# A two-layer SSM/MLP training step on one core: the opening in one written order, half-row forms, and moved gates

## The chip, the cores and the metric

The kernel runs on one core of a Trainium2 chip. The metric is the device time of one launch in microseconds, the median over repeated launches. The kernel before takes 688.93 us (688.62 to 689.18 over three launches). Five engines work side by side: PE (matrix products; its weight loads are listed as PEld), DVE and ACT (elementwise work, reductions, copies out of PSUM, the accumulator memory), POOL (a few small operations and the issue of many transfers) and SP (the issue of transfers only). Each engine executes its own instructions in order and waits on semaphores for what other engines or transfers must have finished.

## The reference

The reference runs four residual blocks on a sequence of 2048 rows with 448 channels in bf16, alternating a long convolution with an MLP, and returns the output and the gradients for eight inputs:

```python
def _A_ref(q, k, v, shift_k, ssm_k, ssm_D):      # D = 448, S = 2048
    k_shift = sum(k_pad[:, t:t + S, :] * shift_k[:, ks - 1 - t] for t in range(4))
    kv = k_shift * v
    y = irfft2(rfft2(pad(kv)) * rfft2(pad(ssm_k)))[:S] + kv * ssm_D
    return q * y

def _B_ref(x, w1, w2):                           # F = 1792
    return einsum(silu(einsum(x, w1)), w2)

x = A_q
x = x + _A_ref(_layernorm(x), A_k, A_v, A_shift_k, A_ssm_k, A_ssm_D)
x = x + _B_ref(_layernorm(x), B_w1, B_w2)
x = x + _A_ref(_layernorm(x), ...)               # same weights
x = x + _B_ref(_layernorm(x), ...)
# outputs: x and the gradients of A_q, A_k, A_v, A_shift_k, A_ssm_k, A_ssm_D, B_w1, B_w2
```

The long convolution's y does not depend on x, only on k, v and the filters, so it is computed once and used in both layers.

## The kernel before

The kernel has three stages.

**Opening** (`_ssm_prefix`). It computes y with a Fourier transform of length 4096 written as matrix products in two stages, 128 by 16 by 2. In order:

- The filter ssm_k (called K) is loaded in four blocks of channels (`KPARTS`), turned on PE (`k_turn`), multiplied with the first-stage matrix `M1sb` (`k_stage1`), turned again in seven groups of 16 blocks (`turn`; groups 5 and 6 by DMA transposes on SP's queue, L444) and multiplied with the second-stage matrix (`spec_k`, `P_`). The result `Ka` is the spectrum of K. It is stored to DRAM (`spec_K`), and a second copy with the real and imaginary halves swapped is made by four SBUF to SBUF transfers for each 2048 columns (`_swap_halves_dma`, L289). Stores and swaps are issued by POOL (`Q` in the written order).
- k is turned (`kT`, L450) and convolved with the four taps of shift_k by products with diagonal matrices (`conv`, L469). Each diagonal is the identity times one column of shift_k, built by sixteen DVE operations (L433). ACT copies the result out (L472), POOL stores it to DRAM (`KS_d`), DVE multiplies it with v (L475), and the product kv goes through the first stage (`stage1_kv`, L485).
- kv is turned in seven groups (`Z_`), taken through the second stage in fourteen blocks of 1024 (`F_`), stored (`spec_KV`), multiplied with the two copies of K's spectrum (`M`, L573), and taken back through the inverse second stage (`V`, L260 and L261). Every PSUM result is copied to SBUF by ACT or DVE (lines L116 and L117 are these copies for all callers).
- `ys` (L604) applies the inverse first stage, eight steps, and leaves y in `Ysb`. It is issued by the main part.

Inside the opening, an order written out by hand (`PRODUCTS`) fixes PE, ACT, DVE and POOL from the ninth block of `spec_k` on; what stands before that is ordered by the planner, which also chooses the copying engine from running loads (`bal.pick`). PSUM gives the opening four tiles of two banks, used in turn.

On SP's queue the opening issues the input loads, the two DMA transposes of K, two DMA transposes that bring w2 turned into `w2T` (L454 and L455), the load of the inverse matrix `Minvsb`, and a tile of grad_out (`gb0`). POOL's queue also carries the loads of w1 and w2 (L563, L564, L568), traced behind the store of the kv spectrum's blocks 9 and 10.

**Main part** (`Main.run`). The rows are handled in four chunks of 512. For each chunk it runs the norms, gates and MLPs forward and then the gradients back. The generators are: `Hh` and `H` (x times w1, with silu and a raw copy `Dall` for its slope), `O` (times w2, added to the residual `X` by DVE, L855), `G` (gradient times w2 turned, copied to `ghT` by ACT or by DVE as `dv` says), `N` (gradient times w1 turned, and the norm's gradient), `T` (turning a tile for the next product). `gate` (L722) multiplies y with the normed tile and adds the residual. `fwd0(c)` norms and gates the chunk c for the first layer; `fwd0_end` finishes its second norm. PE's order here is the order of the text; the other engines are ordered by the planner, with hints: `issue_after` puts an instruction behind another on its engine, `high_priority` moves it ahead. For chunks 1 and 2 the products are woven by one pattern, with L the remaining steps of `fwd0_end`:

```python
weave("OOLOOGOGOGOGGOGTG", O=o, G=g, L=self.norm, T=self.T(...))
```

**Closing** (`_ssm_suffix` and `Jobs`). The gradients of the convolution and the weight gradients of both MLP matrices. `Jobs.last` computes the last block of w1's gradient in two halves of 224 columns, each copied by ACT, turned on PE by `flush` and stored.

Of the kernel before, what the change touches and what calls it, by code (L numbers as in the profile page):

```python
# [17 lines left out]
P = 128  # L18
S = 2048
D = 448  # L20
# [101 lines left out]
PRODUCTS = """  # L122
P9 P10 P11 P12 p9a p10d p11a P13 p12d P8 p8a Z0 Q5 p13d Z1 z0d Z2 z1a Q6 F0 z2d F1 f0a F2 f1d F3 f2a F4 Q4 M0 F5 f3a Z4
f4a Z6 z4d f5a z6d F8 f8a F9 M1 F12 F13 f9a Z5 M2 f12a V0 z5d f13a Z3 v0a F11 z3yd z3xd F7 f11a M3 F6 f7a F10 V1 M4 f6a
V2 f10a M6 V3 v1a M5 V4 v2a M11 V5 v3a V6 M10 v4a V11 M12 v5a V10 M13 v6a V12 v11a M7 V13 v10a M8 V7 v12a M9 V8 v13a v8d
V9 v7a v9a
# [16 lines left out]
def kernel(  # L143
# [33 lines left out]
    k.KS_d = dram.tile([2, P, J, D // 2], BF16, name="KS_d")  # L177
# [87 lines left out]
def _fft_inv_stage2_half(k, pa, pb, B1, ci, psum, cnd):  # L265
    nc = k.nc
    pv = psum.tile([P, 2, 8, 64], FP32, name="ps_v", **k.pt["v"])
    for i in range(8):
        for src, g, first in ((pa, G_IAC, True), (pb, G_IBC, False)):
            for r in range(2):  # L270
                ri = slice(64 * r, 64 * r + 64)
                nc.tensor.matmul(pv[:, r ^ (ci & 1), i, :], lhsT=src[ri, i * P:(i + 1) * P], rhs=k.Gsb[ri, g, ri], start=first, stop=not first)  # L272
    out = (B1[:, :, 32 * ci:32 * ci + 32].rearrange("p q (i h s) -> p h i q s", h=2, s=2) if cnd
           else B1[:, 8 * ci:8 * ci + 8, :].rearrange("p i (q h s) -> p h i q s", h=2, s=2))
    _copy(nc, k.bal.pick(1024), out, pv[:].rearrange("p h i (q s) -> p h i q s", s=2))
# [45 lines left out]
def _ln_steps(k, pool, c, src, si, n_g):  # L321
# [4 lines left out]
    for tl in range(4):  # L326
        k.tc.keep_in_program_order(nc.vector.bn_stats(out=st[:, tl, :], in_=src(tl)))
# [5 lines left out]
        yield  # L333
    for tl in range(4):
        k.tc.keep_in_program_order(nc.vector.tensor_scalar(out=n_g[:, tl, :], in0=src(tl), scalar1=mv[:, tl, 0:1], scalar2=r[:, tl:tl + 1], op0=ALU.subtract, op1=ALU.mult))
        yield
# [6 lines left out]
def _ssm_prefix(k):  # L343
# [4 lines left out]
    with ExitStack() as es:  # L348
# [6 lines left out]
        k.M1sb = k.wk.tile([P, 16, 2, P], BF16, name="M1sb", tag="WX")  # L355
# [8 lines left out]
        kT = k.wk.tile([DC, 4, ND, 4, 129], BF16, name="kT", tag="W1")  # L364
        w2o = k.wk.tile([P, 2 * S + ND * 4 * DC], BF16, name="ksd", tag="W2")
        ksb = [w2o[:, i * S:(i + 1) * S] for i in range(2)]
        ksb += [_hd(k, [P, S], "K_sb")[:] for i in range(2)]
        diag = w2o[:DC, 2 * S:].rearrange("p (c j d) -> p c j d", c=ND, j=4)
        kn = k.wk.tile([P, J, D], BF16, name="k_n", tag="WY")
        vn = k.wk.tile([P, J, D], BF16, name="v_n", tag="WB")  # L370
        skc = spec.tile([DC, ND, 4], FP32, name="skc")
        skb = spec.tile([DC, ND, 4], BF16, name="skb")
# [3 lines left out]
        nc.scalar.dma_start(out=skb[:], in_=k.A_shift_k.rearrange("(c p) j -> p c j", p=DC))  # L376
        m1f = k.M1sb[:].rearrange("p a c k -> p (a c k)")
        for h in range(2):
            for lo, hi in KPARTS[2 * h:2 * h + 2]:
                nc.sync.dma_start(out=ksb[lo // P][:hi - lo], in_=k.A_ssm_k[lo:hi, :])  # L380
            nc.sync.dma_start(out=m1f[:, 2048 * h:2048 * h + 2048], in_=k.m1_h.ap()[:, 2048 * h:2048 * h + 2048])
# [17 lines left out]
        nc.gpsimd.tensor_copy(skc[:], skb[:])  # L399
        def k_turn(lo, hi):  # L400
            n = hi - lo
            kview = ksb[lo // P][:n].rearrange("p (n1 n2) -> p n2 n1", n2=16)
            pt = psum.tile([P, 2, 1024], BF16, name="ps_kt", **a_)
            pv = pt[:, :, 0:8 * n].rearrange("p g (i d) -> p g i d", d=n)
            for i in range(16):
                nc.tensor.transpose(pv[:, i // 8, i % 8, :], kview[:, i, :], k.ident[:n, :n])
            for g, e in enumerate((nc.vector, nc.scalar)):
                last = _copy(nc, e, Kt[:, 8 * g:8 * g + 8, lo:hi], pv[:, g])
                bal.add("act" if g else "dve", 0.9 if g else 0.69)
                if g == 0:  # L410
                    k.kt_copy = last

        def k_stage1(lo, hi, pairs):
            for n2 in pairs:
                ps = psum.tile([P, 2, 2, 256], FP32, name="ps_s1", **k.pt["s1"])
                if n2 == 0:
                    nc.vector.tensor_tensor(out=Kt[0:1, 0, lo:hi], in0=Kt[0:1, 0, lo:hi], in1=Drow[:, lo:hi], op=ALU.add)
                for w in range(2):
                    for c in range(2):
                        nc.tensor.matmul(ps[:, w, c, :hi - lo], lhsT=k.M1sb[:, n2 + w, c, :], rhs=Kt[:, n2 + w, lo:hi], start=True, stop=True)  # L420
                _copy(nc, bal.pick(4 * (hi - lo)), A1K[:, lo // 2:hi // 2, :, n2:n2 + 2, :].rearrange("p b c w s -> p w c b s"),
                      ps[:, :, :, :hi - lo].rearrange("p w c (b s) -> p w c b s", s=2))

        for lo, hi in ((0, 256), (256, D)):
            for plo, phi in KPARTS[lo // P:lo // P + 2]:
                k_turn(plo, phi)
# [1046 lines left out]
```

## Time and profile before

| what | value |
|---|---|
| median of the launches | 688.93 us |
| the profiled execution, its own time | 687.9 us |
| span in the trace | 686.1 us |
| PE busy | 665.3 us, 97% |
| DVE, ACT, POOL busy | 70%, 63%, 15% of the span |
| opening, up to the first product of `ys` | 84.06 us |
| PE idle in the opening | 8.2 us |
| PE idle between 140 and 500 us | 7.0 us |

The span is the time from the first to the last instruction in the trace; the device time has a little more around it. A busy time is the union of an engine's instructions. In a line such as `L889 PE MATMUL ps_n<-w1T,ghT 128*128 128x448 bf16 x448`, L889 is the line of the kernel, then come engine, operation, result and inputs by name, shapes and count. A name with buffers loses its numbers. DMA times run from issue to landing.

### The profile page before, as it was taken

To read this page: it belongs to the slowest core of one execution; us is meant where nothing else is said; L and a number is where in the kernel's file an instruction comes from. 1 tells how busy PE (TensorE), PEld (TensorE's weight loads), DVE (VectorE), ACT (ScalarE), POOL (GpSimd) and SP (SyncE) were. 2 spreads that over 40 slices of the span, in tenths; PEclk is the share of its full clock that TensorE was granted. 3 is DMA by queue.
4 is the path that set the end of the run, shared out by engine and by line. 5 is a ranking of instruction groups with operands and counts; after the bars stand their busy time and mean duration, and the time that the engine had idled before them with its cause. 6 is when DMAs were issued, how large, how long until landed. Compare 5 with 4: busy or idle time off the path is not lost.

```text
span 686.1 us, 14467 instructions
## 1 busy us (share of the span) xinstructions
PE 665.3 (97%) x5844; PEld 362.3 (53%) x5879; DVE 482.2 (70%) x1133; ACT 429.7 (63%) x528; POOL 104.6 (15%) x177
## 2 busy tenths in 40 slices
PE   8989999999999899999899999999999999999997
PEld 6876755554444344444444444544555555555666
DVE  5779954677879858898588874843937554528992
ACT  5988987888758668678477685123634543653431
POOL 1047320110010100101001000010111211102311
PEclk9999999999999999999999999999999999999999
DMA  8999989499788767598776799859599988956981
GB/s 316 248 278 316 342 191 227 112 228 258 191 241 228 219 163 193 123 250 231 182 162 193 218 241 375 241 173 205 200 238 354 324 274 323 351 173 223 324 308 42
DMA packets 203956, 162.60 MB, mean 237 GB/s; under 512 B 153505, under 2 KB 184244, under 8 KB 203122
## 3 DMA queue, kind: packets, MB, share of 16 engines
q1 hardware_dynamic: 190806, 113.35, 61.7%
q0 software_dynamic: 11088, 39.84, 17.1%
q10 hardware_dynamic: 1996, 8.49, 3.8%
q8 instruction: 46, 0.75, 0.4%
q14 instruction: 20, 0.16, 0.1%
HBM read 66.05 MB, written 54.60 MB: 176 GB/s over the span
## 4 chain that ended last, share of the span: by engine, by line
PE 77%; DVE 11%; ACT 5%; DMA 3%; issue 2%; POOL 1%; DVEq 0%; POOLq 0%
PE ps_d L1115 25%; PE ps_n L889 11%; PE ps_o L850 9%; PE ps_g L681 9%; PE ps_h L681 7%; PE ps_v L272 2%; PE ps_g L685 2%; PE ps_h L685 2%; DMA spec_K<-KAB 2%; DVE ln_st L309 1%; ACT KAB L116 1%; DVE lb_v L1063 1%; DMA KAB<-KAB 1%; PE ps_gK L1398 1%; PE ps_y L604 1%
## 5 line engine op out<-in xcount | busy, mean ns | idle before, releaser
L1115 PEld LDWEIGHTS <-dstat 128*128 128x128 bf16 x928 | 87.1, 98 | 75.7 <-issue 4.0
L889 PE MATMUL ps_n<-w1T,ghT 128*128 128x448 bf16 x448 | 94.5, 353 | 0.0
L850 PE MATMUL ps_o<-w2sb,aT 128*128 128x448 bf16 x448 | 89.2, 353 | 1.8 <-DVE X L855 1.8
L116 ACT CAST ghT<-ps_g 128x1024 bf16<-128x1024 f32 (+1 forms) x54 | 48.3, 899 | 60.9 <-PE ps_g L685 46.8
L681 PE MATMUL ps_h<-nT,w1sb 128*128 128x512 bf16 (+1 forms) x410 | 83.0, 336 | 2.1 <-DVE Dall L117 0.8
L681 PE MATMUL ps_g<-nT,w2T 128*128 128x512 bf16 x317 | 77.9, 379 | 1.6 <-ACT Dall L116 0.4
L889 PEld LDWEIGHTS <-ghT 128*128 128x128 bf16 x448 | 42.4, 98 | 45.3 <-issue 4.7
L850 PEld LDWEIGHTS <-aT 128*128 128x128 bf16 x448 | 43.2, 98 | 41.8 <-issue 3.5
L681 PEld LDWEIGHTS <-w1sb 128*128 128x128 bf16 x420 | 39.1, 98 | 37.1 <-issue 8.2
L1063 DVE SCALAR_TENSOR_TENSOR lb_v<-lb_u,n 128x448 bf16<-128x448 bf16 x60 | 37.2, 621 | 27.6 <-ACT lb_u L905 27.2
L833 ACT ACTIVATE aT<-ps_h 128x1024 bf16<-128x1024 f32 (+1 forms) x48 | 44.2, 922 | 19.7 <-PE ps_h L681 11.5
L116 ACT CAST Dall<-ps_h 128x1024 bf16<-128x1024 f32 (+2 forms) x60 | 54.8, 913 | 0.0
L843 ACT ACTIVATE Dall<-Dall 128x1024 bf16<-128x1024 bf16 (+1 forms) x48 | 53.3, 1186 | 0.1
L681 PEld LDWEIGHTS <-w2T 128*128 128x128 bf16 x336 | 31.3, 98 | 40.9 <-issue 5.9
L314 POOL TENSOR_TENSOR rstd<-ln_ve,mhalf 128x2 f32<-128x2 f32 (+1 forms) x24 | 19.6, 818 | 183.7 <-DVE ln_ve L313 183.7
L1115 PE MATMUL ps_d<-X,dstat 128*128 128x448 bf16 x224 | 47.6, 353 | 0.0
L1115 PE MATMUL ps_d<-go,dstat 128*128 128x448 bf16 x224 | 47.2, 353 | 0.0
L1115 PE MATMUL ps_d<-n3m,dstat 128*128 128x448 bf16 (+1 forms) x240 | 47.0, 340 | 0.0
L1115 PE MATMUL ps_d<-n1m,dstat 128*128 128x448 bf16 (+1 forms) x240 | 46.5, 340 | 0.0
L116 ACT CAST A1g<-ps_v 128x1024 bf16<-128x1024 f32 x14 | 14.9, 1064 | 36.5 <-PE ps_v L272 36.5
L855 DVE TENSOR_TENSOR X<-X,ps_o 128x448 bf16<-128x448 bf16 x32 | 19.5, 611 | 18.4 <-PE ps_o L850 18.2
L905 ACT ACTIVATE lb_u<-ps_n,rstd 128x448 bf16<-128x448 f32 x32 | 20.5, 639 | 16.8 <-PE ps_n L889 13.0
(210 smaller groups left out, 1111.9 us busy)
## 6 DMA issues: line engine op xcount, KB each, us to landing
dstat<-a_d SPq DMA_DIRECT2D x28, 512.0 KB, 5.0
dstat<-g_d SPq DMA_DIRECT2D x28, 512.0 KB, 5.4
a_d<-turned SPq DMA_DIRECT2D x16, 512.0 KB, 3.0
g_d<-turned SPq DMA_DIRECT2D x16, 512.0 KB, 3.0
a_d<-turned SPq DMA_DIRECT2D x16, 384.0 KB, 2.7
g_d<-turned SPq DMA_DIRECT2D x16, 384.0 KB, 2.8
spec_K<-KAB POOLq DMA_DIRECT2D x7, 512.0 KB, 6.3
KAB<-KAB POOLq DMA_DIRECT2D x28, 128.0 KB, 5.1
```

Source lines behind the costliest of these rows:

```text
L116: return nc.scalar.copy(out, in_)
L314: nc.gpsimd.tensor_tensor(out=r[:, lo:hi], in0=ve[:, lo:hi], in1=k.mhalf[:, lo:hi], op=ALU.pow)
L681: self.nc.tensor.matmul(ps, lhsT=w[:, b, ft * P:(ft + 1) * P], rhs=x[:, b], start=(start and b == 0), stop=(stop and b == bs[2]))
L685: self.nc.tensor.matmul(ps, lhsT=w[sl, b, ft * P:(ft + 1) * P], rhs=x[sl, b], start=start, stop=stop)
L833: self.last_silu = nc.scalar.activation(aT[hh][:, o:o + hi - lo, :], ps(lo, hi), ACT.Silu)
L843: self.nc.scalar.activation(dT[hh][:, o:o + n, :], dT[hh][:, o:o + n, :], ACT.Derivative_silu)
L850: nc.tensor.matmul(po[:, :D], lhsT=aT[ft // 7][:, ft % 7, tl * P:(tl + 1) * P], rhs=self.w2sb[:, ft, :], start=(ft == 0), stop=(ft == NF - 1))
L855: self.last_o = nc.vector.tensor_tensor(out=X[:, t, :], in0=X[:, t, :], in1=po[:, :D], op=ALU.add)
L889: nc.tensor.matmul(pns[tl][:, :D], lhsT=gh[h][:, ft % 7, tl * P:(tl + 1) * P], rhs=self.w1T[:, ft, :], start=(ft == 0), stop=(ft == NF - 1))
L905: nc.scalar.activation(u0[:], pn[:, :D], ACT.Identity, scale=k.rstd[2 * L + 1][:, t:t + 1], accum_out=cp[:, tl, 0:1])
L1063: nc.vector.scalar_tensor_tensor(out=v[:], in0=u0, scalar=-1.0 / D, in1=n_t, op0=ALU.mult, op1=ALU.mult, accum_out=cp[:, 1:2])
L1115: self.nc.tensor.matmul(ps[:, cols], lhsT=st[:, t, :], rhs=mov[:, t, cols], start=(first and t == 0), stop=(last and t == NT - 1))
```

## The change

- `PRODUCTS` becomes `OPENING`: 272 entries that fix the order of the whole opening behind its first loads, on PE, ACT, DVE, POOL and SP. A capital letter is PE work, a DVE product, a transfer or a norm step; a small letter is the copy out of PSUM, with `a` or `d` for ACT or DVE at its end. The planner's balance between the two copying engines is gone from there.
- Half-row forms (`h` in an entry): a turn or an inverse product is done as pairs of 64-row products (`turned`, `V_`, `_fft_inv_half`). All seven turns of K, two of four of k, six of seven of kv and three of fourteen inverse products have this form.
- The two DMA transposes of K leave SP; PE turns all seven groups.
- The convolution works on half rows too: k is turned in blocks of 128 channels, the diagonals are 64 wide, and each product has 64 rows and 64 columns. The channels are split 256 and 192 in place of 224 and 224. Two broadcast products on DVE build all diagonals. The convolved k is stored in whole rows (`KS_d`), and the closing reads it so.
- w2's DMA transposes come in nine pieces: seven of 256 rows for three blocks, two of 896 rows for the fourth. The inverse matrix and the tile of grad_out follow them on SP.
- The loads of w1 and w2 are traced when the eighth of the eight kv stores has been.
- Main part: the gate and the statistics of the next chunk move out of `fwd0` into `fwd0_end`, behind a residual add; `weave` gets a second L; the load of x for the following chunk moves there too. `G` copies with ACT alone for chunks 1 and 2. In the first chunk the second turned tile is copied by DVE, and another group of tiles has its own PSUM banks.
- Closing: `last` takes 336 columns first and makes the remaining 112 already turned, copied by DVE and stored without a turn.

The core of the diff:

```diff
-PRODUCTS = """
-P9 P10 P11 P12 p9a p10d p11a P13 p12d P8 p8a Z0 Q5 p13d Z1 z0d Z2 z1a Q6 F0 z2d F1 f0a F2 f1d F3 f2a F4 Q4 M0 F5 f3a Z4
...
+OPENING = """
+A0 a0xd A1 a1xd a1ya B01 a0yd b01a G0 G1 B03 b03a A2 a2d B02 A3 D0 B06 b06d B04 b02a a3a B15 b15d B17 T1 t1d b04a T0
+t0d b17a B16 b16a B05 b05a T2h D1 t2d C01 c01a B10 b10d B11 b11a O01 C02 c02a O02 m01 T3h t3d B07 b07a B14 b14a C12
...
+z1d S111 s111d P10 p10a N6 Q4 N7 S110 Z0h z0d Z3h s110a P5 Q6 Z6h z3xa z3yd p5a Q2 F2 f2a F7 z6d M2 F4 F6 f6d F13 f7a
+M7 f4a F12 F0 f13a U13 F1 W1 W2 W4 W0 Q5 M6 f12a f0a Z5 f1a V7 Z4h v7a z5d F3 f3a z4d U6 M13 V2 v2a F10 f10a F9 f9a F5
+M3 f5a V6 U4 v6a F8 f8a U7 M12 V13 v13a F11 f11a M1 U2 V3h U0 v3a V12 M4 V1 M9 M0 V4 V0 v12a M11 v1a v4a v0a V9h V11
+M5 v9a V5 M10 U11 V10 M8 V8h v11d v5a v8a v10d U9
 """
-            for j in range(4):
-                nc.vector.tensor_scalar(out=diag[:, dc, j, :], in0=k.ident[:DC, :DC], scalar1=skc[:, dc, j:j + 1], scalar2=None, op0=ALU.mult)
+        def G_(r):
+            n, rs = 3 + r, slice(64 * r, 64 * r + 64)
+            nc.vector.tensor_tensor(out=diag[rs, 0:n].rearrange("p c j d -> p (c j) d"),
+                                    in0=k.ident[rs, rs].rearrange("p (o d) -> p o d", o=1).broadcast_to((64, 4 * n, 64)),
+                                    in1=skb[rs, 0:n].rearrange("p c (j o) -> p (c j) o", o=1).broadcast_to((64, 4 * n, 64)), op=ALU.mult)
+        def turned(key, name, srcs, half):
+            if half:
+                pt = bank(key, [P, 2, 16, 64], name, BF16)
+                for i in range(16):
+                    _turn64(k, pt, i, srcs(i))
...
-        for g in range(5, 7):
-            nc.sync.dma_start_transpose(out=Z[:, 16 * g:16 * g + 16, :], in_=A1Kf[:, 16 * g:16 * g + 16, :].rearrange("p a b -> p (a b)"))
-                    for t in range(4):
-                        nc.tensor.matmul(pc[:, u, e * DC:(e + 1) * DC], lhsT=src, rhs=diag[:, 2 * h + e, t, :], start=(t == 0), stop=(t == 3))
+                        for r in range(2):
+                            if (e, r) in at:
+                                rs = slice(64 * r, 64 * r + 64)
+                                nc.tensor.matmul(pc[:, at[e, r], u, :], lhsT=src[rs], rhs=diag[rs, e, q, :], start=(q == 0), stop=(q == 3))
-        nc.sync.dma_start_transpose(out=k.w2T[:, 0:3, :], in_=k.B_w2[:, 0:384])
-        w2t = nc.sync.dma_start_transpose(out=k.w2T[:, 3:4, :], in_=k.B_w2[:, 320:448])
+        def W(i):
...
+                for lo in range(0, F, 256):
+                    nc.sync.dma_start_transpose(out=k.w2T[:, 0:3, lo:lo + 256], in_=k.B_w2[lo:lo + 256, 0:384])
...
+                for lo in range(0, F, 896):
+                    nc.sync.dma_start_transpose(out=k.w2T[:, 3:4, lo:lo + 896], in_=k.B_w2[lo:lo + 896, 320:448])
+        def U_(lo):
+            hi = min(x for x in (2, 4, 6, 7, 9, 11, 13, 14) if x > lo)
+            nc.gpsimd.dma_start(out=k.SPEC_d["KV"][:, lo * 1024:hi * 1024], in_=zkv(lo * 1024, hi * 1024))
+            stored.add(lo)
+            if len(stored) == 8:
+                ...
+                nc.gpsimd.dma_start(out=k.w1sb[:, 0:3, :], in_=k.B_w1[0:384, :].rearrange("(c p) f -> p c f", p=P))
+        with tc.manual_schedule(engines={e.engine for e in (nc.tensor, nc.scalar, nc.vector, nc.gpsimd, nc.sync)}):
@@ main part
-            self.a_fwd(c, 0, xc, n00, ((0, 4),))
+            _ln(k, self.ch, c, xc, 0, n00)
-            norm = _ln_parts(k, self.ch, c, self.xs(c), 1, n01, ((0, 4),))
-            next(norm)
-            self.norm = self.fwd0_end(c, norm, n01)
+            self.norm = self.fwd0_end(c, xc, n00, n01)
+    def fwd0_end(self, c, xc, n00, n01):
+        norm = _ln_parts(self.k, self.ch, c, self.xs(c), 1, n01, ((0, 4),))
+        with self.tc.issue_after(self.last_o.ins) if c > 1 else nullcontext():
+            self.gate(c, xc, n00)
+            next(norm)
+        if c < 3:
+            self.x_load(c + 1)
+        yield
-        hs = [self.Hh(0, 0, nT, aT, dT1, 0, (1, 3), (1,)), self.Hh(0, 0, nT, aT, dT1, 1)]
+        hs = [self.Hh(0, 0, nT, aT, dT1, 0, (1, 2), (2,)), self.Hh(0, 0, nT, aT, dT1, 1)]
-            self.transp_half(self.n0[0][1], nT, GBLK, 1)
+            self.transp_half(self.n0[0][1], nT, GBLK, 1, nc.vector)
-                g = self.G(gT, gh2, dv=(1, 4))
+                g = self.G(gT, gh2, dv=(1, 4) if c == 3 else ())
-                    weave("OOLOOGOGOGOGGOGTG", O=o, G=g, L=self.norm, T=self.T(self.n0[c + 1][1], nT, GBLK))
+                    weave("OOLOOLGOGOGOGGOGTG", O=o, G=g, L=self.norm, T=self.T(self.n0[c + 1][1], nT, GBLK))
@@ closing, Jobs.last
+        cols = slice(0, 3 * DC)
...
+                nc.tensor.matmul(ps[:DC, 0:P], lhsT=movs[i]()[:, t, 3 * DC:D], rhs=sts[i][:, t, :], start=(i == 0 and t == 0), stop=(i == 1 and t == NT - 1))
...
+        nc.vector.tensor_copy(o7[:, 3], ps[:DC, 0:P])
```

More of the change, by code (lines that the diff above doesn't have):

```diff
@@ L434, in _ssm_prefix, with a @@
[L434 to L443 removed]
+        def a(part, s, e):
+            lo, hi = KPARTS[part]
+            n = hi - lo
+            pv = live["a", part][:, :, 0:8 * n].rearrange("p g (i d) -> p g i d", d=n)
+            gs = {"": slice(0, 2), "x": slice(0, 1), "y": slice(1, 2)}[s]
+            _copy(nc, e, Kt.rearrange("p (g i) d -> p g i d", g=2)[:, gs, :, lo:hi], pv[:, gs])
@@ L539, in Q, with Z_ @@
             _swap_halves_dma(k, KAB[:, 0, :], Ka, lo, hi)
-        def Z_(g):
-            pt = live["z", g] = psum.tile([P, 16, P], BF16, name="ps_tr", **a_)
-            for i in range(16):
-                nc.tensor.transpose(pt[:, i, :], B1[:, 16 * g + i, :], k.ident[:])
-        def z(g, part, eng):
-            lo, hi = (8 * part, 8 * part + 8) if g == 3 else (0, 16)
-            _copy(nc, eng, block(g, lo, hi), live["z", g][:, lo:hi, :])
+        def Z_(g, half):
+            turned(("z", g), "ps_tr", lambda i: B1[:, 16 * g + i, :], half)
```

357 lines of the change are left out of this document (180 added, 177 removed).

## The prediction

> **What bounds the kernel now.** First the page's head and busy times, then the table of stretches:
>
> ```profile
> span 686.1 us, 14467 instructions
> PE 665.3 (97%) x5844; PEld 362.3 (53%) x5879; DVE 482.2 (70%) x1133; ACT 429.7 (63%) x528; POOL 104.6 (15%) x177
> ```
>
> ```profile
> 0.00:84.06 84.06, 75.90 (x1100) 61.47 (x1107) 67.53 (x95) 69.60 (x73) 30.95 (x64) 1.00 1.04 299
> 30.00:42.00 12.00, 11.42 (x191) 9.74 (x190) 9.24 (x17) 9.94 (x12) 3.25 (x6) 1.00 1.25 182
> 70.00:84.06 14.06, 13.33 (x243) 12.33 (x241) 13.55 (x13) 13.38 (x15) 5.27 (x10) 1.00 1.00 343
> 140.00:500.00 360.00, 353.05 (x2094) 164.71 (x2118) 271.28 (x767) 234.88 (x295) 31.23 (x48) 1.00 0.80 215
> ```
>
> The columns are length, then PE, PEld, DVE, ACT, POOL, the granted clock, DMA share, GB/s. Over the whole span PE idles 686.1 - 665.3 = 20.8 us. Of that, 84.06 - 75.90 = 8.2 us lie in the opening, which ends at 84.06 where ps_y starts, and 360 - 353.05 = 7.0 us in the main part. In the opening PE, ACT and DVE are busy 75.9, 69.6 and 67.5 us: three engines close together, PE first. From 70 us on DVE and ACT are full as well. The clock is 1.00, so the throttle has no part in it. The main part is PE end to end; only its PE waits and its work can give anything.
>
> The chain of waits (start, length, what) shows a second pace-maker in the opening, the transfers that swap the spectrum's halves:
>
> ```profile
> 18.67 3.73 PE ps_kT L450 x64
> 56.03 6.30 DMA spec_K<-KAB
> 69.63 7.34 DMA KAB<-KAB
> 83.00 1.02 ACT A1kv L116
> 84.06 6.74 PE ps_y L604 x32
> ```
>
> The last swap lands at 69.63 + 7.34 = 76.97; seven microseconds of products and copies later ps_y starts. So the end is set by engines and by DMA almost together.
>
> **The opening, priced by groups of instructions.** Groups of the opening, forms apart (count | busy, mean ns | idle before):
>
> ```profile
> L469 PE MATMUL ps_cv<-ksd,kT 112*128 112x112 bf16 x256 | 13.9, 213 | 0.4 <-ACT KAB L116 0.3
> L544 PE MATMUL ps_tr<-ident,A1kv 128*128 128x128 bf16 x112 | 7.1, 219 | 0.3 <-ACT KAB L116 0.2
> L232 PE MATMUL ps_tr<-ident,KAB 64*128 64x64 bf16 x160 | 3.0, 190 | 0.2 <-issue 0.2
> L260 PE MATMUL ps_v<-Gpre,pab 128*128 128x128 bf16 x112 | 13.2, 219 | 0.2
> L472 ACT CAST ks_kv<-ps_cv 128x896 bf16<-128x896 f32 x8 | 7.3, 914 | 3.8 <-PE ps_cv L469 3.8
> L116 ACT CAST KAB<-ps_s 128x1024 bf16<-128x1024 f32 x12 | 12.1, 1041 | 1.2 <-PE ps_s L251 0.7 <-PE ps_s L485 0.2 <-PE ps_s L420 0.2
> L116 ACT COPY KAB<-ps_tr 128x2048 bf16<-128x2048 bf16 x3 | 5.6, 1890 | 0.0
> L117 DVE CAST KAB<-ps_s 128x1024 bf16<-128x1024 f32 x10 | 11.9, 1217 | 1.6 <-PE ps_cv L469 1.2 <-PE ps_s L420 0.4
> L117 DVE COPY ZkvB<-ps_tr 128x2048 bf16<-128x2048 bf16 x3 | 3.6, 1218 | 0.4 <-PE ps_tr L544 0.4
> L433 DVE TENSOR_SCALAR ksd<-ident,skc 112x112 bf16<-112x112 bf16 x16 | 2.8, 242 | 0.0
> ```
>
> PE. A half-row transpose of 64x64 advances at 3.0 us / 160 = 0.019 us, because the two row halves run side by side; a full one at 7.1 / 112 = 0.063. With these two paces: the convolution's 256 products (13.9 us) become 4 x 64 + 4 x 48 = 448 half-row products of 64 columns, 8.4 us: -5.5. The key's 64 transposes (3.73 us) become 32 full and 64 half: 2.0 + 1.2 = 3.2, -0.5. Seven turns of K in place of five (the two DMA turns go): 224 half transposes for 160, +1.2. Seven turns of kv: one full, six half: 1.0 + 3.6 for 7.1, -2.5. Three of fourteen inverse products half-row: each 0.6 us for 13.2 / 14 = 0.94, -1.0. Together -8.3. What it costs is the change of form, which this trace shows in the main part:
>
> ```profile
> 95.60 1.48 PE L681 MATMUL ps_h<-nT,w1sb 128*128 128x256 bf16 x12
> 97.02 0.39 PE L685 MATMUL ps_h<-nT,w1sb 64*128 64x256 bf16 x3
> 97.34 0.50 PE L681 MATMUL ps_h<-nT,w1sb 128*128 128x256 bf16 x3
> ```
>
> Twelve steps of 0.11 us from 95.60 reach 96.92; the half-row ones start at 97.02: 0.1 us per change. The new order has 21 half-row stretches, so 42 changes, 4.2 us; now there are about 7, 0.7. PE net: -8.3 + 3.5 = -4.8 us. The bounds are -8.3 (no cost of change) and 0 (a half-row product of the convolution no faster than the 13.9 row's 0.054 us, which excludes most of the gain).
>
> ACT and DVE. I count elements per partition read from PSUM. fp32 reads: ACT 57,216 now, 66,560 after, so +9,344, at 1.041 us per 1024: +9.5. bf16 reads on ACT fall from 15,872 to 3,072: -12,800 at 1.890 per 2048: -11.8. ACT net -2.3. DVE: -9,344 fp32 at 1.217 per 1024 = -11.1; bf16 from 24,064 to 40,960, +16,896 at 1.218 per 2048 = +10.0; the sixteen diagonal builds (2.8) become two broadcast products of 768 and 1024 elements, which no row shows: 1.1 us at the bf16 rate, 2.1 us at the fp32 rate, I take 1.6, halfway, since no row is nearer: -1.2. DVE net -2.3. So the transposed bf16 goes to the engine that reads it at 0.59 ns an element, the fp32 to the one that reads it at 1.02, and both lose a little.
>
> I take -4.8 us for the opening: PE is the busiest of the three, and the 3.8 us that ACT waits for ps_cv hang on its longest step. Ends: 0 and, if the fixed order also halves the 8.2 us of idle, -8.9.
>
> DMA queues. SP now:
>
> ```profile
> 19.75 6.82 SPq L444 DMA_TRANSPOSE KAB<-KAB  x2
> 26.67 7.02 SPq L454 DMA_TRANSPOSE w2T<-in_B_w_dram  x1
> 33.73 3.42 SPq L455 DMA_TRANSPOSE w2T<-in_B_w_dram  x1
> 37.20 0.59 SPq L218 DMA_DIRECT2D Minvsb<-c_minv  x1
> ```
>
> SP loses L444 and gets nine pieces. L454 moves three 128-column blocks in 7.02 us and L455 one in 3.42: 1.62 us fixed and 1.80 per block of 1792 rows. Seven pieces of 256 rows x 3 blocks: 7 x (1.62 + 0.77) = 16.7; two of 896 rows: 2 x 2.52 = 5.0; 21.8 us. Nothing but the key's transposes must precede them, and their place in the text orders only SP's own queue. Those ended at 22.4; I take a start near 20 us, an end near 42, against 37.2 now. Behind them wait only Minv and the gradient tile, wanted at ps_y, some 35 us later: nothing. Covered as long as they do not slow the swaps, which start at about the same time (a rival below).
>
> POOL: the same seven spectrum stores and 28 swaps come before all but one of the kv stores, at nothing. The w1 loads stay behind all eight kv stores, as now:
>
> ```profile
> 77.60 0.78 POOL L563 DMA_DIRECT2D w1sb<-in_B_w_dram  x1 [0.50 <-issue]
> w1sb<-in_B_w_dram POOLq DMA_DIRECT2D x1, 1344.0 KB, 12.2
> 94.52 0.83 PE L681 MATMUL ps_h<-nT,w1sb 128*128 128x256 bf16 x6
> ```
>
> They land at 89.8, 4.7 us ahead of use. With an opening 4.8 us shorter use is at 89.7; the last kv chunk is copied early in the new order, so I let the issue move up as much: nothing. If it does not move, the margin is just gone and each further microsecond costs one. The convolution result stored in whole rows: nothing, it lies beside other work at both ends.
>
> **Main part.** What PE waits for after the opening:
>
> ```profile
> PE ps_g L685 <- DVE ghT L117: 3.1, 2, 1.6
> PE ps_o L850 <- DVE X L855: 1.8, 2, 0.9
> PE ps_h L681 <- DVE Dall L117: 0.8, 1, 0.8
> PE ps_h L681 <- ACT Dall L116: 0.6, 1, 0.6
> ```
>
> Chunks 1 and 2: the ghT copy that DVE makes late (3.1) goes to ACT, so the wait goes; four copies of 1 us join an ACT that is busy 234.88 of 360. The residual add that PE waits for (1.8) stands on DVE behind the gate and the statistics of the next chunk; both are moved behind it, so this wait goes too. What is late next is that chunk's norm:
>
> ```profile
> 326.02 1.31 DVE L317 TENSOR_SCALAR n<-X,ln_mv,rstd 128x448 bf16<-128x448 bf16 x4 [1.81 <-POOL rstd L314]
> 335.93 0.63 PE L658 MATMUL ps_t<-ident,n 64*128 64x64 bf16 x32
> ```
>
> It is done at 327.3 and read at 335.9: 8.6 us of cover, and the move costs some 5 us of it. I take -4.5 of the 4.9, the rest for restarts; ends 0 and -4.9. First chunk: nT's second copy goes from ACT to DVE and the third group of tiles, not the second, gets its own banks; of 0.8 + 0.6 I take -1.0; ends +0.5 and -1.4. The reload of x for the next chunk goes later with the gate that frees it, a chunk ahead of use: nothing.
>
> Tail. After the last product now:
>
> ```profile
> 682.10 0.34 ACT L1130 CAST dout<-ps_d 128x224 bf16<-128x224 f32 x1 [2.33 <-PE ps_d L1115]
> 682.49 0.32 PE L1220 MATMUL ps_dt<-ident,dout 128*112 128x128 bf16 x2 [0.43 <-ACT dout L1130]
> 682.85 0.29 DVE L117 COPY wts<-ps_dt 112x256 bf16<-112x256 bf16 x1 [2.33 <-PE ps_dt L1220]
> ```
>
> The fourth block is now produced already turned, so ACT's copy and PE's turn leave: 682.85 - 682.10 = 0.75; PE's columns grow from 64 x 224 to 32 x (336 + 128), by 512, some 0.2 us at the 0.48 ns a column of the ps_cv row (13.9 us / 256 / 112). The hand-overs of the two steps that leave give about that back, so I take -0.7; ends 0 and -0.8.
>
> Sum: 4.8 + 4.5 + 1.0 + 0.7 = 11.0 us. This execution took 687.9 (span 686.1), so 676.9; the median 688.93 stands 1.0 above it, so 677.9, rounded to 678.
>
> **Rivals.** Copies bind, PE's relief is hidden: ACT and DVE are each full from 70 us, and each loses only 2.3. Then the opening gives 2.3, the sum is 8.5, time 680.4. For it: 13.55 and 13.38 of 14.06 busy; against it: ACT's 3.8 us on ps_cv. [...]
>
> Nine pieces choke the swaps, slower than before. While DMA transposes run the trace moves 182 GB/s, against 343 later. The chain from first spectrum store to last swap takes 35 us now and is DMA-paced. If a piece costs nearer the 3.4 us of one L444 transpose (6.82 / 2) than 2.4, nine take up to 31 us and end near 51, 14 us later than now. The main part and tail give 6.2 back, so this decides once the pieces hold the chain more than 7.6 us longer, that is past 45 us. At 2.9 us a piece they end at 46 to 47, and with queueing behind them the chain ends about 10 us later: 688.9 + 10 - 6.2, about 692.
>
> The order packs better than I take: the opening's idle halves, -4.1 more, 674. And the main part's waits come back (the moved gate delays norm and transposes as much as it frees): only opening and tail count, 683.
>
> **How the numbers follow.** Forecast 678: 0.43. Copies bind 680: 0.16. Tighter order 674: 0.10. Main part gives nothing 683: 0.06. Nine pieces 692: 0.25, of which 0.05 come out near the time before. A kernel like this can be told from no change from about 0.2%, 1.4 us, on: faster 0.75, same 0.05, slower 0.20. The range: down to 673.5 for the tighter order, up to 690, where the slower case is left out. The forecast's own range is 674 to 683.
>
> **What the changed profile would show.** ps_y starts near 79 us; convolution near 8.4 us of PE for 13.9; ACT's wait for ps_cv well under 3.8; the last w2T piece issued before 45 us; the last swap landed by about 72; no PE wait on w1sb. PE waits on ghT and X, 4.9 us now, under 0.5 in chunks 1 and 2. One copy and no turn after the last product. Wrong if DVE's products wait for swaps later than now, if ps_y does not start before 82, or if a new PE wait on nT or ps_t stands in chunks 1 and 2.

## The result and the profile after

The changed kernel takes 683.64 us (median of 6 runs, 681.56 to 684.93) against 688.30 before (6 runs, 687.87 to 689.18): ratio 0.9929, interval 0.9912 to 0.9946. It is faster by 4.7 us, not by 10.9. The profiled execution took 684.05 us, its span is 682.3.

Where the forecast missed is seen by cutting the span where ps_y starts. The table of stretches of the changed kernel (columns as in the prediction), the main part first, then the opening by finer cuts up to ps_y:

```profile
85.80:140.00 54.20, 53.41 (x372) 29.84 (x376) 33.45 (x81) 42.46 (x54) 6.73 (x9) 1.00 0.77 193
140.00:500.00 360.00, 357.87 (x2121) 167.18 (x2145) 267.35 (x761) 242.10 (x303) 32.83 (x51) 1.00 0.82 219
```

```profile
0.00:22.60 22.60, 19.94 (x350) 15.45 (x350) 13.84 (x17) 13.18 (x15) 2.54 (x10) 1.00 0.92 326
22.60:42.00 19.40, 15.42 (x501) 11.86 (x504) 15.06 (x25) 16.08 (x18) 6.72 (x10) 1.00 1.13 201
42.00:54.00 12.00, 7.74 (x103) 5.14 (x96) 5.96 (x7) 5.91 (x8) 6.04 (x12) 0.72 0.90 299
54.00:85.81 31.81, 28.32 (x592) 21.49 (x595) 31.02 (x31) 31.66 (x36) 18.16 (x33) 1.00 0.86 275
sum 85.81, PE 71.41 PEld 53.94 DVE 65.88 ACT 66.84 POOL 33.45; mean PE 17.85 PEld 13.48 DVE 16.47 ACT 16.71 POOL 8.36
```

From ps_y to the end of the span the kernel got shorter: 686.1 - 84.06 = 602.0 before, 682.3 - 85.81 = 596.5 now, 5.5 us, close to the 4.5 + 1.0 + 0.7 = 6.2 of the forecast. In the main part PE's idle time fell from 7.0 to 2.1 us. The opening got *longer*: ps_y starts at 85.81, not near 79. Yet all three engines lost work, as forecast: PE 75.90 to 71.41, ACT 69.60 to 66.84, DVE 67.53 to 65.88. So PE is idle 14.4 us of the opening instead of 8.2, and the stretch 42 to 54 us shows where: 7.74 of 12 us busy, at a granted clock of 0.72.

The timeline of PE there, and at 22 us (start, length, group; in brackets the idle time ahead of it and what ended it):

```profile
22.65 0.20 PE L508 MATMUL ps_cv<-M1sb,kT 64*128 64x64 bf16 x1
25.06 1.11 PE L508 MATMUL ps_cv<-M1sb,kT 64*128 64x64 bf16 x47 [2.21 <-issue]
...
41.70 0.64 PE L238 MATMUL ps_tr<-ident,KAB 64*128 64x64 bf16 x31
46.55 0.23 PE L238 MATMUL ps_tr<-ident,KAB 64*128 64x64 bf16 x1 [4.21 <-issue]
46.71 1.04 PE L533 MATMUL ps_s<-ks_kv,M1sb 128*128 128x256 bf16 x4
```

PE stops after 1 of the 48 products of one group and after 31 of the 32 transposes of another. The products on both sides of each stop read and write the same tiles, so no copy and no load can release them; the releaser is "issue", nothing that the profile shows. PE's waits in the opening, grouped (what waited and on which line, what ended the wait: us in all, times, longest), hold 7.8 us of this kind. The last row is the largest group before the change, a wait for a copy:

```profile
PE ps_tr L238 <- issue: 4.2, 1, 4.2
PE ps_cv L508 <- issue: 2.2, 1, 2.2
PE ps_s L533 <- issue: 1.4, 2, 0.8
```

```profile
PE ps_s L420 <- DVE KAB L117: 1.3, 2, 0.8
```

In the second stop the granted clock falls to half. This row of the table of stretches is cut at the clock's own steps:

```profile
44.13:50.96 6.83, 4.41 (x43) 2.69 (x44) 3.05 (x3) 2.77 (x3) 1.80 (x4) 0.50 1.01 311
```

PE's products of 512 columns (L257) start 0.43 us apart there, and 0.21 at a clock of 1.00; so 4.41 us of work at half pace are 2.2 us lost, by this estimate. Stops and half clock make 10.0 us of the opening.

### The profile page after: what moved, and what is told of

Read it like the earlier page. It is cut to its first block, busy times and chain, and to the rows that moved or that the text cites. A ratio compares the mean times of both kernels' runs of the same rounds, so it can differ in the third digit from the quotient of the medians.

```text
span 682.3 us, 15297 instructions
## 1 busy us (share of the span) xinstructions
PE 660.2 (97%) x6273; PEld 353.5 (52%) x6310; DVE 479.0 (70%) x1113; ACT 428.5 (63%) x529; POOL 105.7 (15%) x176
## 4 chain that ended last, share of the span: by engine, by line
PE 88%; ACT 5%; issue 2%; DMA 2%; DVE 1%; SPq 0%; POOL 0%; DVEq 0%; ACTq 0%
PE ps_d L1161 25%; PE ps_n L936 13%; PE ps_o L897 12%; PE ps_h L727 11%; PE ps_g L727 10%; PE ps_h L731 2%; PE ps_v L278 2%; PE ps_g L731 2%; PE ps_cv L508 1%; DMA K_sb<-in_A_ssm_k_dram 1%; PE ps_gK L1451 1%; PE ps_y L650 1%; ACT Dall L890 1%; PE ps_gkv L1422 1%; ACT KAB L116 1%
## 5 line engine op out<-in xcount | busy, mean ns | idle before, releaser
L1161 PEld LDWEIGHTS <-dstat 128*128 128x128 bf16 x896 | 84.2, 98 | 76.9 <-issue 4.0
L116 ACT CAST ghT<-ps_g 128x1024 bf16<-128x1024 f32 (+1 forms) x58 | 52.2, 906 | 51.8 <-PE ps_g L731 38.5
L727 PEld LDWEIGHTS <-w1sb 128*128 128x128 bf16 x420 | 39.0, 98 | 36.2 <-issue 7.3
```

The source lines that it names most:

```text
L116: return nc.scalar.copy(out, in_)
L727: self.nc.tensor.matmul(ps, lhsT=w[:, b, ft * P:(ft + 1) * P], rhs=x[:, b], start=(start and b == 0), stop=(stop and b == bs[2]))
L1161: self.nc.tensor.matmul(ps[:, cols], lhsT=st[:, t, :], rhs=mov[:, t, cols], start=(first and t == 0), stop=(last and t == NT - 1))
```

## The experiments

**The two halves apart.** main_only joins the old opening to the new main part and tail, open_only the new opening to the old main part.

> The opening of the kernel before (whole-row products, two DMA turns, w2's transposes in two pieces) with the changed kernel's main part and tail. Theory (the main part and tail gave what was forecast, the opening ate half of it): ps_y starts at 84 us as before, the rest is 5.5 us shorter (602.04 to 596.5 us in the two profiles), time 682.8 us. Rival (the main part's gain hangs on the new opening, since w1 and w2 are issued 9 us earlier by it): a gain of 2 us or less, 686 us or more.

> The changed opening with the main part of the kernel before. Theory: ps_y starts at 85.8 us, PE stops of 2 and 4 us with 'issue' as releaser in the middle of a group stand at 22.9 and 42.3 us again, time 688.3 + 1.75 = 690 us. Rival (the opening's loss belongs to the first chunk's weights or to one execution): ps_y near 79 to 84, time below 688.3 us.

Measured: main_only 681.21 us, ratio 0.9897 (0.9882 to 0.9912), ps_y at 84.4; open_only 689.11 us, 1.0011 (0.9998 to 1.0025), ps_y at 85.0 in its profile. The main part and tail give 7.0 us without the new opening's help; the opening gives nothing or loses. In open_only the stops stand at the same two products (1.75 and 2.86 us). The halves, 7.0 won and 0.9 lost, make 6.1 us, and the two together gave 4.7; the difference is not explained.

**Fewer instructions.** The theory: PE's instructions arrive in blocks, here called pages, and PE stops when a page is used up before the next is there. The profile's summary counts 46 packets on the instruction queue before and 49 after. all_full_forms lets every T, K, Z and V of the order string (turns of k, of K, of kv, and inverse products) use the full form (cut at `...`):

```
-... T2h D1 t2d ... K0h k0d ... Z2h z2d ... V3h U0 v3a ...
+... T2 D1 t2d ... K0 k0d ... Z2 z2d ... V3 U0 v3a ...
```

> The changed kernel with all eighteen half-row turns and inverse products (T, K, Z, V) in the full 128x128 form: 288 matmuls and 288 weight loads fewer in the opening, 128 of each ahead of the second stop. More PE work: turns at 16 x 0.063 us for 0.62, inverse products 0.94 for 0.6, +7 us, less 36 changes of form at 0.1 us. Theory (PE stops because its instructions run out, 256 a page): the second page border falls about 256 instructions later, the 4.2 us stop goes or shrinks below 2 us, and with it the 6.8 us at half clock; ps_y near 82 us, time 679 to 681 us. Rival (PE stops because of the order of the work or the DMA traffic): the stop at 42 us stays, the PE work is added, ps_y near 89 us, time 687 us.

Measured: 678.94 us, ratio 0.9866 (0.9849 to 0.9884). The stretches of all_full_forms that answer to those above:

```profile
22.60:42.00 19.40, 18.64 (x428) 15.67 (x430) 17.11 (x26) 17.98 (x20) 8.69 (x13) 1.00 1.12 218
42.00:54.00 12.00, 11.76 (x172) 9.44 (x173) 11.21 (x14) 10.92 (x13) 6.29 (x12) 1.00 1.03 319
54.00:79.80 25.80, 23.29 (x332) 18.89 (x334) 23.94 (x22) 24.94 (x27) 15.14 (x29) 1.00 0.98 328
sum 79.80, PE 73.23 PEld 59.53 DVE 65.80 ACT 66.69 POOL 32.66; mean PE 18.31 PEld 14.88 DVE 16.45 ACT 16.67 POOL 8.16
```

ps_y starts at 79.80, where the prediction had it, with *more* PE work than the changed kernel: 73.23 against 71.41 - 2.2 = 69.2 at full clock, so +4.0 (expected 7 - 3.6 = 3.4). Of the stops one of 0.51 us is left, and the clock is 1.00. The sum closes: 85.81 - 10.0 + 4.0 = 79.8. The rival, by which the second stop stays, is out; what transfers add to it is tested below.

**Borders moved.** pad_61 makes 71 warm-up products out of 10 (three of 512 columns become 64 of 64 columns): 61 more, and no other edit.

```
-        for _ in range(10):
-            nc.tensor.matmul(pw[:], lhsT=zero[:, 0:P], rhs=zero[:], ...)
+        for i in range(71):
+            nc.tensor.matmul(pw[:, 0:512 if i < 7 else 64], lhsT=zero[:, 0:P], rhs=zero[:, 0:512 if i < 7 else 64], ...)
```

> The changed kernel with 71 warm-up products (7 of 512 columns, 64 of 64) in place of 10: 61 matmuls, up to 122 instructions, more ahead of all other PE work, in time in which PE waits for the first load. Theory (page borders of 256 instructions): the stops move back by about 122 instructions: the first from the second product of C12 to about the 41st of C02, or a border with slow work behind it; the second out of K5h to about the start of K2h. Rival (a wait that the profile does not show, tied to the work itself): both stops stay where they are, after the first product of C12 and in the last transposes of K5h. Time within 2 us of the changed kernel by both.

```profile
22.30 0.82 PE L508 MATMUL ps_cv<-M1sb,kT 64*128 64x64 bf16 x44
24.45 0.47 PE L508 MATMUL ps_cv<-M1sb,kT 64*128 64x64 bf16 x20 [1.34 <-issue]
```

This is C02, a group of the convolution, which now stops after its 44th product; the old place is behind the first product of the group C12. Between them lie 20 products of C02, 32 of T3, 8 of B07 and B14 (first stage of K) and the first of C12: 61, just as many as were put ahead. The stop is tied to the count of instructions and not to the work. The second did not come out where expected: four stops of 0.36 to 0.86 us took its place, and the time is 680.69 us, 3.0 less than the changed kernel (expected: within 2). Where the borders fall is by itself worth microseconds.

**The supply by itself.** stream issues idle products in three streams ahead of the opening: 1024 half-row, 512 full, 1024 half-row. It ran once (771.24 us) and is read for its profile alone.

```
+        for part, n in enumerate((1024, 512, 1024)):
+            for i in range(n):
+                rs = slice(0, P) if part == 1 else slice(64 * (i % 2), 64 * (i % 2) + 64)
+                w = P if part == 1 else 64
+                o = i // 2 % 4 * w
+                nc.tensor.matmul(pw[:, i % 2, o:o + w], lhsT=zero[rs, 0:P], rhs=zero[rs, 0:w], ...)
```

> all_full_forms with three streams of idle products ahead of the opening, in the place where PE warms up: 1024 half-row ones (64x64, eight pages of 256 instructions with their weight loads), 512 full ones of 128 columns (four pages), 1024 half-row ones again. The first stream runs beside the opening's loads, the last with most of them landed. Theory: a page is used in 128 x 0.019 = 2.4 us by half-row products and in 128 x 0.063 = 8.1 us by full ones, while the queue brings one in some 4 to 5 us: the first and third stream take 8 x 4 to 5 = 32 to 40 us instead of 19.5, in bursts of 128 products with stops between, and the full one takes 32 us without a stop. If DMA traffic makes the stops, the first stream has them and the third has not. Rival (the stops are not the instruction queue's): 19.5, 32 and 19.5 us without stops. The rest of the kernel is as in all_full_forms, later by the sum.

PE's timeline of stream (a group joins what runs without a stop):

```profile
5.41 3.29 PE L413 MATMUL ps_w<-zero 64*128 64x64 bf16 x213
13.97 3.60 PE L413 MATMUL ps_w<-zero 64*128 64x64 bf16 x128 [5.26 <-issue]
20.16 3.60 PE L413 MATMUL ps_w<-zero 64*128 64x64 bf16 x128 [2.60 <-issue]
...
39.63 32.72 PE L413 MATMUL ps_w<-zero 64*128 64x64 bf16 x768 [1.69 <-issue]
73.75 2.04 PE L413 MATMUL ps_w<-zero 64*128 64x64 bf16 x128 [1.41 <-issue]
77.48 2.04 PE L413 MATMUL ps_w<-zero 64*128 64x64 bf16 x128 [1.69 <-issue]
81.21 2.04 PE L413 MATMUL ps_w<-zero 64*128 64x64 bf16 x128 [1.69 <-issue]
```

The wait is the instruction supply. 2560 products with a weight load each are 5120 instructions; the queue's packets went from 47 in all_full_forms to 67, twenty more: 256 instructions a page. In the third stream half-row products run in bursts of exactly 128, 2.04 us of work and then 1.69 (twice 1.41) of stop, which is a page every 3.73 us (twice 3.45). In the middle 512 full products, with 128 half-row ones on either side, run 32.72 us without a stop: (32.72 - 2 x 2.04) / 512 = 56 ns a product. The DMA engines have next to nothing else to do by then, as the last two numbers of the stretch say (share and GB/s):

```profile
30.00:96.60 66.60, 50.56 (x1888) 49.21 (x1880) 0.00 (x0) 0.00 (x0) 0.00 (x0) 1.00 0.01 3
```

Beside the opening's loads the first pages came later, with stops of 5.26 and 2.60. The expected 4 to 5 us a page was too much for a quiet queue and too little for a full one. The packet records of the traces tie each stop to its page: in every stop of 1 us or more with the releaser "issue", in the opening of every run, PE resumes 1.2 to 1.6 us after a packet of the instruction queue has ended. In the third stream a packet begins 1.0 to 1.4 us after a burst has begun and takes 0.9 to 1.25, so the wait for the next page is only partly covered by 2.04 us of work: at 16 ns a product (2.04 us / 128) each border of the third stream costs 1.4 to 1.7 us.

**What makes a page late.** two_pieces is all_full_forms with w2's transposes in two pieces, as before the change (cut at `...`; the fourth block's two pieces become one in the same way):

```
-                for lo in range(0, F, 256):
-                    nc.sync.dma_start_transpose(out=k.w2T[:, 0:3, lo:lo + 256], in_=k.B_w2[lo:lo + 256, 0:384])
+                nc.sync.dma_start_transpose(out=k.w2T[:, 0:3, :], in_=k.B_w2[:, 0:384])
...
```

> all_full_forms with w2's transposes in the two pieces of the kernel before (10.4 us of SP) in place of nine (14.4 us). Prediction's step: the nine pieces cost nothing, 679 us. Rival (many pieces hold the spectrum's swaps, or many small pieces let them pass): over 1 us either way.

Measured: 684.87 us (683.93 to 685.19), ratio 0.9947 (0.9932 to 0.9962), 5.9 more than all_full_forms. In its timelines of PE and SP the stops are back:

```profile
31.55 0.56 PE L478 MATMUL ps_tr<-ident,KAB 128*128 128x128 bf16 x7 [1.75 <-issue]
39.94 0.71 PE L478 MATMUL ps_tr<-ident,KAB 128*128 128x128 bf16 x5 [3.39 <-issue]
22.70 9.41 SPq L612 DMA_TRANSPOSE w2T<-in_B_w_dram  x1
32.16 4.61 SPq L614 DMA_TRANSPOSE w2T<-in_B_w_dram  x1
```

Here they stand between full transposes. In the packet records the page ahead of 31.55 began at 27.93 and took 2.31 us, where 0.9 to 1.1 is usual. The page ahead of 39.94 took 1.14 us but began only at 37.50, 0.95 us after PE had stopped; what held it the records don't show. The stops make 5.1 us, and the 2.5 us of work in the half clock that begins in the second lose some 1.3; ps_y is at 86.6, 6.8 later. With one edit between the two kernels the long pieces are the cause: the nine short ones, which I had priced at nothing, are worth 5.9 us in this order.

late_w2 was to hold the nine pieces back with an ordering edge:

```
+                with tc.issue_after(live["pc", 11].ins):
+                    nc.sync.dma_start_transpose(out=k.w2T[:, 0:3, 0:256], ...)
```

> The changed kernel with w2's nine transposes, and Minv and the gradient tile behind them, held back until the copy of P11 (about 52 us), so that SP's queue moves nothing between 22 and 52 us. Theory A (pages of instructions come late because of this traffic): the stops at 22.9 and 42.3 us shrink towards the 1.7 us that the quiet stream showed, ps_y near 82 us, time 680 us. Theory B (half-row groups use a page faster than it comes even with a quiet queue): the stops stay at 1.5 to 4 us, time 682 to 685 us. By both the late w2 costs nothing by itself: nine pieces of 1.6 us end near 67 us.

It measured 683.74 us and told neither theory: the transposes started at 23.8 us all the same, so the edge did not make SP wait. It stands as a repeat of the changed kernel (second stop 5.04 us; in its profile the first one is not there). hold_after makes them wait for data: k and v change places in memory, so w2T takes v's.

```
-        kn = k.wk.tile([P, J, D], BF16, name="k_n", tag="WY")
-        vn = k.wk.tile([P, J, D], BF16, name="v_n", tag="WB")
+        kn = k.wk.tile([P, J, D], BF16, name="k_n", tag="WB")
+        vn = k.wk.tile([P, J, D], BF16, name="v_n", tag="WY")
```

> The changed kernel with one edit: the tiles of k and v change places in memory, so that w2T takes v's, which is read until about 56 us, and the nine transposes with Minv and the gradient tile behind them cannot start before; between 22 and 56 us SP's queue moves nothing (in late_w2 they had started at 23.8 us all the same). Theory A (the pages come late because of this traffic): both stops shrink below 2 us or go, no half clock, ps_y near 80 us, time 678 to 680 us. Theory B (half-row groups use a page faster than it comes, whatever the traffic): stops of 2 and 4 us stay, ps_y near 85 us, 682 to 685 us. By both, transposes that end near 71 us and Minv behind them are still in time for ps_y.

> full_turns (T and K turns in the full form) with the same exchange of tiles, so w2's transposes start at about 52 us. Theory A and B both: full_turns has no stop left, so nothing is gained before 52 us beyond 1 us: 677.5 to 678.5 us. Rival (the transposes now meet the swaps and the kv stores): 680 us or more, swaps landing past 72 us.

Measured: 724.75 and 719.48 us, ratios 1.0504 (1.0450 to 1.0558) and 1.0441 (1.0382 to 1.0501). Both theories missed what came behind; only the rival put down for hold_full_turns named it. First the question itself, in PE's waits of hold_after up to 60 us. Its profiled execution was the longest of its four (733.94 us), but up to 60 us its granted clock is 1.00:

```profile
PE ps_tr L238 <- issue: 1.8, 1, 1.8
PE ps_cv L508 <- issue: 1.5, 1, 1.5
```

With nothing on SP's queue the stop at 42.3 us is gone; the one at C12 is 1.5 us for 2.2, and the 1.8 us one stands at 52.8, where the transposes run again. So theory A holds for the size and B for the rest: without the traffic a border still cost 1.5 and 1.8 us, about what it did in the quiet stream (1.41 to 1.69), with it up to 5.04 (late_w2). Then the price. SP's timeline of the changed kernel, then that of hold_after, then its waits from 50 us on:

```profile
21.88 10.72 SPq L613 DMA_TRANSPOSE w2T<-in_B_w_dram  x7
32.64 3.60 SPq L616 DMA_TRANSPOSE w2T<-in_B_w_dram  x2
```

```profile
48.86 35.94 SPq L613 DMA_TRANSPOSE w2T<-in_B_w_dram  x7
84.85 19.86 SPq L616 DMA_TRANSPOSE w2T<-in_B_w_dram  x2
```

```profile
PE ps_v L266 <- DVE pab L580: 27.0, 4, 13.0
PE ps_t L704 <- DMA gb<-in_grad_out_dram: 23.6, 1, 23.6
DVE pab L580 <- DMA KAB<-KAB: 18.5, 2, 14.6
```

Seven pieces that took 10.72 us of SP in the changed kernel take 35.94 beside the swaps, and between 48 and 110 us a swap takes 14.4 us to land (median) for 5.2. The products wait for the swaps, and the turns of the gradient tile (ps_t), which stand ahead of ps_y on PE, wait for that tile, whose load stands behind the pieces. hold_full_turns shows the same against full_turns: 32.58 us for 10.73, a swap 12.1 for 4.7, and waits of 14.4 and 27.9 for the first two rows. In the changed kernel the last transpose is off SP at 36.2 us and the first swap is issued at 39.55; so they spare each other.

**Where half-row forms pay.** full_turns gives only T and K the full form.

> The changed kernel with only the nine half-row turns of T and K in the full form; the Z turns and inverse products (V) of the last 35 us of the opening stay half-row. Theory (instructions run out where half-row groups follow each other closely): all those stops lay ahead of 47 us, so none comes back; against all_full_forms 6 x 0.4 + 3 x 0.34 us of PE work less and 18 changes of form more (1.8 us), ps_y near 78.5 us, time 677 to 678.5 us. Rival (half-row forms cost by themselves, wherever they stand): half of the gain of all_full_forms or less, 681 us or more.

Measured: 678.28 us (677.78 to 679.15), ratio 0.9852 (0.9837 to 0.9867), ps_y at 80.1. It beats both kernels, and by its spread can't be told from all_full_forms: PE's work fell by 1.2 us (73.23 to 72.05), ps_y did not move. The stops ahead of 47 us are gone, but against the expectation one came elsewhere, right ahead of ps_y, after 13 of the 32 half-row turns of the gradient tile. The chain of waits has it:

```profile
71.57 6.43 ACT A1kv L116 x7
78.40 1.35 issue
79.75 0.46 PE ps_t L704 x19
```

The copies that ps_y reads end at 79.25 here and at 79.16 in all_full_forms. So the stop cost at most 0.9 us, and the copies allowed no more than that. The last stretches of full_turns show the copying engines:

```profile
54.00:66.00 12.00, 11.04 (x152) 7.00 (x154) 11.34 (x11) 12.00 (x15) 9.39 (x19) 1.00 0.99 308
66.00:80.00 14.00, 11.10 (x263) 10.03 (x262) 13.25 (x12) 12.90 (x15) 7.68 (x13) 1.00 0.98 339
```

ACT is busy 12.00 of 12 us from 54 us on and 12.90 of the 14 behind, DVE 13.25 of those 14; there PE has time to spare, and half-row forms buy little or nothing.

**The main part, step by step.** dv_only makes one edit in the kernel before; dv_back undoes it in all_full_forms; tail_only takes over only the last weight gradient's products.

```
-                g = self.G(gT, gh2, dv=(1, 4))
+                g = self.G(gT, gh2, dv=(1, 4) if c == 3 else ())
```

> The kernel before with one edit: the ghT copies of chunks 1 and 2 go to ACT, none to DVE. Prediction's step: PE's two waits for them, 3.1 us in all, go: 688.3 - 3.1 = 685.2 us. Rival (the wait moves to the residual add or the norm that stand on DVE, or to ACT's queue): 687 us or more, with a new PE wait in chunks 1 and 2.

> all_full_forms with the ghT copies of chunks 1 and 2 put back on DVE (groups 1 and 4), as in the kernel before. Prediction's step: PE waits 3.1 us for them again, in two places of up to 1.6 us: 678.9 + 3.1 = 682.0 us. Rival (the wait had only moved, or the moved gate had already freed DVE): no change, 679 us.

> The kernel before with only the last weight gradient's products changed: one product group of 336 columns and one of 112 that comes out turned, in place of two of 224, so that ACT's copy and PE's turn after the last product leave. Prediction's step: -0.7 us, 687.5 us (ends 0 and -0.8). Rival (the end hangs on the stores' landing): no change, 688.2 us.

Measured: dv_only 685.08 us (684.66 to 686.02), ratio 0.9955 (0.9939 to 0.9972), 3.1 us less, as the row of 3.1 said. Its waits after the opening are those of the prediction without the first:

```profile
PE ps_o L850 <- DVE X L855: 1.8, 2, 0.9
PE ps_h L681 <- DVE Dall L117: 0.8, 1, 0.8
PE ps_h L681 <- ACT Dall L116: 0.6, 1, 0.6
```

dv_back is 689.13 us, 10.2 above all_full_forms, not 3.1 us. Its timeline of PE shows the two waits doubled, at 232 and 326 us:

```profile
232.38 0.39 PE L731 MATMUL ps_g<-nT,w2T 64*128 64x512 bf16 x2 [3.00 <-DVE ghT L117]
326.65 0.61 PE L731 MATMUL ps_g<-nT,w2T 64*128 64x512 bf16 x2 [2.99 <-DVE ghT L117]
```

The moved gate, with the statistics and the norm of the next chunk, stands on DVE ahead of that copy (in chunk 1 from 223.3 to 231.1 us), so copy and gate had to move together. With each of the two waits the granted clock is halved, 3.41 and 6.83 us long. The waits, 6.0 us, and half of PE's 8.8 us of work in the halved stretches, 4.4, make 10.4 of the 10.8 between the two profiled executions. tail_only is 687.98 us, ratio 0.9995 (0.9986 to 1.0003): 0.3 us less, from none to 1.0. The forecast 0.7 lies in that interval, and so does nothing.

## Why the prediction was right and wrong

The direction held, and 683.64 lies in the wide range of 673.5 to 690; the size did not hold, and the forecast's own range of 674 to 683 was missed by 0.6. That the measured time is nearly that of the rival "main part gives nothing, 683" is chance: the main part gave what was forecast, and the opening gave nothing. By its own terms:

- **Opening, -4.8: wrong, +1.75,** outside its ends of 0 and -8.9. The sums of work came out close (PE -4.5, ACT -2.8, DVE -1.7 for -4.8, -2.3, -2.3). For PE that is in part luck: without the 2.2 us of half clock it is -6.7, and which term was too small is not shown. (The 0.1 us per change of form explains little of it: in all_full_forms 36 changes fewer were worth 7 - 4.0 = 3.0 us, 0.08 each.) The step that failed is the sentence "I take -4.8 us for the opening: PE is the busiest of the three". It let PE's idle 8.2 us stand and asked only what half-row products cost in PE, at the 0.019 us pace of short groups. (The two row halves do run side by side in that trace: the half-row turns behind 24.04 us start in pairs 3 ns apart, a pair every 29 ns.) At that pace a page of 128 products and their loads is gone in 2.4 us; in the opening before, packets of the instruction queue come at least 5.3 us apart, so that trace had never asked for pages so fast, and no row of it priced that. The runs showed 7.8 us of stops, in which PE waits for its instructions, and 2.2 of half clock in its place. all_full_forms, nearly without them, has the opening at 79.8.
- **Nine pieces "nothing": wrong.** They took 10.72 + 3.60 = 14.3 us, not 21.8, and ended at 36.2, so the rival in which they choke the swaps did not come about; its mechanism is real, but only a part of the 41 us that each hold run lost against its own base (724.75 - 683.64, 719.48 - 678.28): in hold_full_turns PE waits 14.4 us for DVE's products behind the swaps and 27.9 for the gradient tile behind the pieces. What I had not thought of is that instruction pages come late beside long pieces: 5.9 us in two_pieces.
- **Copies bind (rival): true in part,** from 54 us on, as full_turns indicates. It was not what decided.
- **Main part, -4.5 and -1.0: right.** The waits on ghT, X and Dall are gone from the changed kernel; a 0.5 us wait on ACT's copy is new. The norm that was to be late next made no wait. With the tail main_only gives 7.0 us for 6.2 forecast.
- **Tail, -0.7: open.** One DVE copy of 0.29 us is left after the last product, as foretold; the gain is too small to be told from none.
- **No PE wait on w1sb: right.**
- **The signs:** "if ps_y does not start before 82" was the one that came true. The convolution's products sum to 9.7 us of PE for the 8.4 foretold; in full_turns, with the clock at 1.00, to 9.0. ACT's wait for ps_cv fell from 3.8 to 2.6, but 6.1 us of waiting for ps_s came beside it. The last swap is issued at 71.2, so it can't have landed by 72 (the quickest transfer of KAB there took 3.0 us): it is late with the rest of the opening.

Not settled: why the second stop is 2.86, 4.21 and 5.04 us long in three kernels with the same opening (open_only, the changed one, late_w2). The packet behind it begins 0.56, 1.80 and 2.71 us after PE has stopped, then takes 0.93 to 0.97, and PE resumes 1.4 to 1.5 later; so the lengths differ by the packet's start, and what delays that start is open. So is how many pages the supply keeps ahead.

## What to carry to other kernels

Count instructions as well as microseconds: when an edit replaces few long products by many short ones, multiply their time each by 128 (a page of stream held 128 products with their loads) and compare with the time from one instruction page to the next in a trace (3.73 us in the quiet stream, where the stops were 1.41 to 1.69 us; beside the opening's loads they were 2.60 and 5.26). Slow products were no safeguard: in two_pieces PE stopped for 1.75 and 3.39 us between full transposes. An "issue" wait in the middle of a group whose neighbours use the same tiles is the sign. A transfer priced at nothing because its result is wanted late may still hold up what moves at the same time (a swap took 14.4 us beside the late pieces of hold_after, for 5.2), so its place in time and the size of its pieces belong in the sum.

## What the runs showed of the hardware beyond that

A long stop of PE cost more than its length in these runs: behind the one of 4.21 us another 2.2 us, by the estimate above. With each stop of 2.86 us and more, whatever PE waited for (2.86, 2.99, 3.00, 3.39, 4.21, 5.04, 5.26, and the long ones of the hold runs), the granted clock went to 0.50 for at least 3.41 us, beginning in the stop or at most 1.4 us behind it. After the one of 2.21 it stayed at 1.00, and so it did through the quiet stream's stops of 1.41 to 1.69, until 1.5 us behind the last of them, where it was halved for 6.83 us. Four more times it was halved behind shorter stops (1.06, 1.55, 1.75 and, in hold_full_turns, 2.15). The halved stretches ahead of the kernel's end are 3.41 us long or whole multiples of it, as the 6.83 us row above.

A DMA transpose of 256 rows took 1.5 us of SP ahead of the swaps (10.72 / 7 in the changed kernel) and 5.1 beside them (35.94 / 7 in hold_after; in hold_full_turns 32.58 / 7 = 4.7), and the swaps took 14.4 us (12.1) for 5.2 (4.7) meanwhile.
